# Attention with windowed and global tokens, then expert layers: loads in 64-row halves on ScalarE's queue, gate transposes in the score banks, VectorE copies later

## The chip, the core and the metric

The kernel runs on one core of one Trainium2 chip. The core has five engines with a queue each: TensorE (PE in the profile; PEld is its weight load), VectorE (DVE), ScalarE (ACT), GpSimd (POOL) and SyncE (SP). Each works through its own instructions in order and waits on semaphores of the others. Transfers between HBM and SBUF can be issued by SP, ACT and POOL; the profile shows 16 DMA engines behind them.

The metric is the device time of one execution in microseconds; of several runs the median is taken. Before the change it is 766.53 us, the median of 3 runs (766.46 to 770.74).

## What is computed

Two parts follow one another. The first is an attention over 8 batches of 8 heads: 512 local tokens see the 32 global tokens and a window of 32 tokens to each side, and 32 global tokens see everything. The second sends each of the 4,352 resulting rows to one of 8 experts with a fixed capacity.

```python
s_g = scale * q_g @ concat(k_g, k_l).T             # 32 global queries, all keys
out_g = softmax(s_g) @ concat(v_g, v_l)
s_ll = where(abs(i - j) <= 32, scale * q_l @ k_l.T, -1e9)
s_l = concat(scale * q_l @ k_g.T, s_ll)
out_l = softmax(s_l) @ concat(v_g, v_l)
x = concat(out_g, out_l) as [B*S, H*D]
logits = x @ w_gate                                # greedy assignment, cap = N // E
out[rows of e] = relu(x[rows of e] @ w1[e]) @ w2[e]
```

The diff touches the attention part alone. The expert part starts when all of x and all gate logits are there.

## The kernel before

Inputs are laid out on the host so that a pair of heads is one transfer. The tile `qk` of a pair has 128 partitions, 64 for each head (the head dimension), and holds transposed queries and keys. The tile `vw` has the keys of a window on the 128 partitions, and for each head 16 windows of values with a column of ones. There are 32 pairs, four to a batch. Both tiles have 6 buffers.

The work of a batch is a list of units: two `Local` units for each pair (one for each head) and two `Glob` units (one for four heads). Their order is pair 0, pair 1, Glob 0, pair 2, pair 3, Glob 1, in the last batch pair 0, Glob 0, Glob 1, pairs 1 to 3. There are 80 units. A unit goes through four stages:

- `a`: scores by matmul into PSUM tiles called S (4 buffers). A pair does both of its heads at once with 64 small matmuls (line 160); a Glob does 16 (line 183).
- `e`: on DVE, four passes over the scores that add the mask and find the extreme (line 114), then on ACT four exponentials (line 117). A Glob has two DVE reductions and three exponentials.
- `c`: transposes of the probabilities on PE into PSUM tiles T (2 buffers; line 122, for a Glob line 212), and an evacuation to SBUF by `evac`, which gives three of four to ACT (line 241) and every fourth to DVE (line 243).
- `d`: matmuls with the values into PSUM tiles O (2 buffers; line 131, for a Glob line 222), and on DVE the division by the sum.

The order is written out by hand in one loop (line 327). Iteration i issues, in this order: loads, stores that have come due, `a` of unit i+2 (if it begins a pair or is a Glob), `c` of unit i, `e` of unit i+2, `d` of unit i-1, and then one or more gate steps of an earlier batch. Since every engine keeps program order, what is issued first on an engine runs first there.

Loads before: `load_qk` issues on SP and `load_v` on POOL, whole tiles of 128 partitions. Three qk and two vw tiles are issued ahead of the loop, and the `while` at line 333 then issues as many as the pair index of unit i+2 plus 4 allows, the Globs counting as later pairs. A load whose buffer is still in use waits on its queue, SP or POOL.

The gate: for each finished batch, four steps transpose 128-column blocks of the attention output (`gate_x`, line 249), one multiplies with the gate weights (`gate_m`, line 255) and one transposes back and sums into the logits (`gate_l`, line 264). Before the change the transposes of `gate_x` land in O tiles, except in the last batch, where they land in S tiles.

Of the kernel before, what the change touches and what calls it, by code (L numbers as in the profile page):

```python
# [8 lines left out]
F32 = mybir.dt.float32  # L9
# [9 lines left out]
B, H, SL, SG, D = 8, 8, 512, 32, 64  # L19
S = SL + SG  # L20
# [5 lines left out]
NB = SL // 128  # L26
NW = SL // 32
NP = H // 2
QW = SL + SG
KW = 27 * 32  # L30
# [33 lines left out]
def attention(ctx, tc, A, consts, xd, ident, L, nbatch, rt=None):  # L64
    nc = tc.nc
    ac = ctx.enter_context(tc.tile_pool(name="ac", bufs=1))
    ld = ctx.enter_context(tc.tile_pool(name="ld", bufs=3))
    wk = ctx.enter_context(tc.tile_pool(name="wk", bufs=3))
    ps = ctx.enter_context(tc.tile_pool(name="ps", bufs=2, space=PSUM))

    G = [(b, g) for b in range(nbatch) for g in range(2)]
    qk, vw, xs = {}, {}, {}

    def load_qk(b, p):
        t = ld.tile([128, QW + KW], F32, name="qk", bufs=6)
        nc.sync.dma_start(t, A["qk"][b, p])
        qk[b, p] = t

    def load_v(b, p):
        t = ld.tile([128, 2, NW, D + 1], F32, name="vw", bufs=6)  # L80
        nc.gpsimd.dma_start(t.rearrange("p h w d -> p (h w d)"), A["vw"][b, p])
        vw[b, p] = t

    pg = [ac.tile([128, 6, 128], F32, name=f"pg{i}") for i in range(2)]
    mask = ac.tile([128, NB, 128], F32, name="mask")
# [1 line left out]
    P = [(b, p) for b in range(nbatch) for p in range(NP)]  # L87
# [3 lines left out]
    wt = ps.tile([128, NB, 128], F32, name="T", bufs=2)  # L91
    for _ in range(WARM):
        nc.tensor.matmul(wt[:, 0, :], warm, warm, start=True, stop=True)
    load_qk(0, 0)
    nc.sync.dma_start(mask.rearrange("p a b -> p (a b)"), A["mask"])
    nc.sync.dma_start(ident, A["ident"])
    for i in range(2):
        nc.gpsimd.memset(pg[i], 0.0)
    load_v(0, 0)
    load_qk(0, 1)  # L100
    nc.sync.dma_start(wg.rearrange("p a b -> p (a b)"), A["wg"])
    load_v(0, 1)
    load_qk(0, 2)
    later = []

    class Local:
# [3 lines left out]
        def e(s):  # L110
            s.p = wk.tile([128, NB, 128], F32, name="p", bufs=4)
            nm = wk.tile([128, NB], F32, name="nm", bufs=4)
            for c in range(NB):
                nc.vector.tensor_tensor_reduce(s.p[:, c, :], s.st[:, c, :], mask[:, c, :], -SCALE, BIG,  # L114
                                               ALU.add, ALU.min, nm[:, c:c + 1])
            for c in range(NB):
                nc.scalar.activation(s.p[:, c, :], s.p[:, c, :], AF.Exp, bias=nm[:, c:c + 1], scale=-1.0)  # L117

        def c(s):
            t = ps.tile([128, NB, 128], F32, name="T", bufs=2)  # L120
            for c in range(NB):
                nc.tensor.transpose(t[:, c, :], s.p[:, c, :], ident)  # L122
            s.pt = wk.tile([128, NB, 128], F32, name="pt", bufs=3)
            evac(s.pt, t)

        def d(s):
            b, q, h = s.b, s.q, s.h
            o = ps.tile([128, NB, D + 1], F32, name="O", bufs=2)
            for c in range(NB):
                for r in range(4):  # L130
                    nc.tensor.matmul(o[32 * r:32 * r + 32, c, :], s.pt[:, c, 32 * r:32 * r + 32],  # L131
                                     vw[b, q][:, h, 4 * c + r, :], start=True, stop=True)
            ls = wk.tile([128, NB], F32, name="ls", bufs=4)
            nc.vector.tensor_scalar(ls, o[:, :, D], 1e-9, None, op0=ALU.add)
            nc.vector.reciprocal(ls, ls)
            if q + h == 0:
                xs[b] = wk.tile([128, NB, DM], F32, name="xs", bufs=2)
            hd = D * (2 * q + h)
            nc.vector.tensor_tensor(xs[b][:, :, hd:hd + D], o[:, :, 0:D],
                                    ls[:, :, None].to_broadcast([128, NB, D]), op=ALU.mult)  # L140
            if q == NP - 1 and h == 1:
                later.append(lambda: nc.sync.dma_start(
                    ap_of(xd, (b * S + SG) * DM, [[DM, 128], [128 * DM, NB], [1, DM]]), xs[b]))
# [19 lines left out]
    class Glob:  # L163
# [43 lines left out]
        def c(s):  # L207
            s.pt = wk.tile([128, 6, 128], F32, name="pgt", bufs=2)
            for lo, n in ((0, 4), (4, 2)):
                t = ps.tile([128, NB, 128], F32, name="T", bufs=2)  # L210
                for k in range(n):
                    nc.tensor.transpose(t[:, k, :], s.p[:, lo + k, :], ident)  # L212
                evac(s.pt[:, lo:lo + n], t[:, :n])

        def d(s):
            b, g = s.b, s.g
# [17 lines left out]
            later.append(put)  # L234

    nev = [0]

    def evac(dst, src):
        nev[0] += 1
        if nev[0] % 4 < 3:  # L240
            nc.scalar.activation(dst, src, AF.Copy)
        else:
            nc.vector.tensor_copy(dst, src)

    def gate_x(src, xt, c, spare):
        t = ps.tile([128, NB, 128], F32, name="S" if spare else "O", bufs=4 if spare else 2)
        n = src.shape[1]
        for k in range(n):
            nc.tensor.transpose(t[:, k, :], src[:, k, c * 128:(c + 1) * 128], ident)  # L249
        evac(xt[:, c, :n * 128], t[:, :n].rearrange("p a b -> p (a b)"))  # L250

    def gate_m(xt, n):
        lt = ps.tile([128, 512], F32, name="O", bufs=2)
        for c in range(4):
            nc.tensor.matmul(lt[32 * c:32 * c + 32, :n * 128], wg[:, c, :], xt[:, c, :n * 128],
                             start=True, stop=True)
        ltc = wk.tile([128, 512], F32, name="ltc", bufs=2)
        evac(ltc[:, :n * 128], lt[:, :n * 128])
        return ltc

    def gate_l(ltc, J, n):
        t = ps.tile([128, NB, 4, 32], F32, name="T", bufs=2)
        for k in range(n):
            nc.tensor.transpose(t[:, k].rearrange("p a b -> p (a b)"), ltc[:, k * 128:(k + 1) * 128], ident)
        nc.vector.tensor_reduce(L[:, J:J + n, :], t[:, :n, :, 0:8].rearrange("p k c e -> p k e c"),
                                axis=AX.X, op=ALU.add)

    def gate_units(b, src, J, n):
        xt = []

        def go(c):
            if c == 0:
                xt.append(wk.tile([128, 4, 128 * n], F32, name=f"xt{n}", bufs=2))
            if c < 4:
                gate_x(src(), xt[0], c, b == nbatch - 1)
            elif c == 4:
                xt.append(gate_m(xt[0], n))
            else:
                gate_l(xt[1], J, n)
        return [lambda c=c: go(c) for c in range(6)]  # L280
# [9 lines left out]
    units, heads = [], {}  # L290
# [8 lines left out]
    for b in range(nbatch):  # L299
# [3 lines left out]
        lo = gate_units(b, lambda b=b: xs[b], 4 * b, NB)  # L303
# [5 lines left out]
        else:  # L309
            for k, f in enumerate(lo):  # L310
                extra.setdefault(s0 + (k if b == nbatch - 2 else GS[k]), []).append(f)
            if gl:
                extra.setdefault(s0 + 2, []).append(lambda b=b: load_gx(b // 4))
                for k, f in enumerate(gl):
                    extra.setdefault(s0 + 10 + k, []).append(f)
    nl = [3]

    def pairidx(u):
        if isinstance(u, Local):
            return u.b * NP + u.q  # L320
        return u.b * NP + 2 * u.g + 1

    nu = len(units)
    first = rt.setup(slice(0, 28)) if rt else None
    LA = 2
    due = []
    for i in range(-LA, nu + 3):
        if rt and i == 2:
            rt.load()
        if rt and i == 12:  # L330
            rt.prepare()
        if i + LA < nu:
            while nl[0] < len(P) and nl[0] <= pairidx(units[i + LA]) + 4:
                load_qk(*P[nl[0]])
                load_v(*P[nl[0] - 1])
                nl[0] += 1
                if nl[0] == len(P):
                    load_v(*P[-1])
            while later and due[0] <= i:
                later.pop(0)()  # L340
                due.pop(0)
            if i + LA in heads:
                heads[i + LA].a()
        if 0 <= i < nu:
            units[i].c()
        if i + LA < nu:
            units[i + LA].e()
        if 1 <= i <= nu:
            units[i - 1].d()
        while len(due) < len(later):  # L350
            due.append(i + 2 if i < nu - 10 else i)
        while i >= nu - 10 and later:
            later.pop(0)()
            due.pop(0)
        for f in extra.get(i, []):
            f()
        if rt and i >= nu - 3:
            for _ in range(6):
                next(first, None)
# [45 lines left out]
class Routing:  # L405
# [6 lines left out]
    def load(s):  # L412
        s.cf = s.consts.tile([128, CF], F32, name="cf")
        s.nc.sync.dma_start(s.cf, s.A["cf"])
# [586 lines left out]
```

## Time and profile before

| | |
|---|---|
| median of 3 runs | 766.53 us (766.46 to 770.74) |
| the profiled execution | 772.81 us |
| its span, first to last instruction | 771.0 us |
| PE busy | 680.0 us, 88% |
| DVE busy | 478.1 us, 62% |
| ACT busy | 319.1 us, 41% |
| POOL busy | 130.2 us, 17% |
| moved by DMA | 120.37 MB |

The profiled execution is one run, 6.3 us longer than the median. Times inside it are counted from its first instruction. The profile has these views: busy time of each engine; the span in 40 slices; the DMA queues; the chain of waits that ended last; groups of equal instructions with their mean time; waits by engine and by what ended them; a timeline; and windows, where for any stretch the busy time of each engine, the number of its instructions (x), the granted clock of PE (PEclk, 1.00 is full speed), the busy share of the 16 DMA engines and what they moved stand in one row. "Issue" as the cause of a wait means that the engine waited for nothing that the profile shows.

### The profile page before, as it was taken

How to read it: one execution, taken by the hardware profiler on the slowest of the kernel's cores; microseconds unless marked ns; L12 is line 12 of the kernel's file. 1: busy time of each engine (PE TensorE's matmuls, PEld its weight loads, DVE VectorE, ACT ScalarE, POOL GpSimd, SP SyncE). 2: the span in 40 equal slices, each digit the busy share in tenths (PEclk: the TensorE clock that was granted, in tenths of full speed). 3: DMA queues.
4: the chain of work that ended last, by engine and by line, in shares of the span. 5: the costliest groups of instructions: out<-in, count | busy, mean ns of one | idle time of the engine just before them, and what ended most of it. 6: DMA issues, size and time to landing. Idle time of an engine off the chain costs nothing.

```text
span 771.0 us, 23101 instructions
## 1 busy us (share of the span) xinstructions
PE 680.0 (88%) x9788; PEld 543.9 (71%) x9788; DVE 478.1 (62%) x1742; ACT 319.1 (41%) x823; POOL 130.2 (17%) x150
## 2 busy tenths in 40 slices
PE   6768898888889428999999999999999999989997
PEld 5446665556657217968877977877877886977985
DVE  2566566566657678877777676776776775542410
ACT  3447566565657104434333333342423433442420
POOL 2000010010000013043042033024015014411001
PEclk8889899899999759999999999999999999999999
DMA  9985587776841124062062054045035035513001
GB/s 348 413 336 227 225 318 305 259 288 269 310 169 23 57 103 174 2 249 86 2 260 76 2 186 149 3 130 191 14 111 198 29 111 184 178 45 134 22 14 44
DMA packets 27815, 120.37 MB, mean 156 GB/s; under 512 B 6208, under 2 KB 6464, under 8 KB 19520
## 3 DMA queue, kind: packets, MB, share of 16 engines
q0 software_dynamic: 14848, 85.47, 30.0%
q1 hardware_dynamic: 12864, 33.43, 11.4%
q8 instruction: 77, 1.26, 0.7%
q14 instruction: 26, 0.21, 0.1%
HBM read 101.06 MB, written 17.83 MB: 154 GB/s over the span
## 4 chain that ended last, share of the span: by engine, by line
PE 74%; DVE 15%; issue 7%; ACT 2%; DMA 2%; SPq 0%; POOLq 0%; DVEq 0%; ACTq 0%
PE Y L885 23%; PE H L857 18%; PE S L160 5%; PE T L122 5%; PE O L131 5%; PE R L469 4%; DVE r_G L401 3%; DVE w2l L401 3%; PE S L183 2%; PE H L732 2%; PE O L249 2%; PE O L222 2%; PE Y L875 2%; DVE r_pm L401 2%; PE T L212 1%
## 5 line engine op out<-in xcount | busy, mean ns | idle before, releaser
L857 PE MATMUL H<-xh,w1h 128*128 128x272 f32 x512 | 151.2, 295 | 8.0 <-DVE hl L401 7.8
L857 PE MATMUL H<-xh,w1l 128*128 128x272 f32 x512 | 150.5, 294 | 0.0
L857 PE MATMUL H<-xl,w1h 128*128 128x272 f32 x512 | 150.0, 293 | 0.0
L859 ACT ACTIVATE hh<-H 128x272 fp32r<-128x272 f32 x128 | 50.9, 398 | 136.9 <-PE H L857 120.4
L857 PEld LDWEIGHTS H<-xh,w1h 128*128 128x128 f32 x512 | 96.4, 188 | 12.5 <-DVE hl L401 7.1
L885 PE MATMUL Y<-w2h,hh 128*128 128x512 f32 x256 | 103.8, 405 | 0.0
L885 PE MATMUL Y<-w2h,hl 128*128 128x512 f32 x256 | 102.9, 402 | 0.0
L885 PE MATMUL Y<-w2l,hh 128*128 128x512 f32 x256 | 102.5, 400 | 0.0
L857 PEld LDWEIGHTS H<-xl,w1h 128*128 128x128 f32 x512 | 96.5, 188 | 0.7
L857 PEld LDWEIGHTS H<-xh,w1l 128*128 128x128 f32 x512 | 96.4, 188 | 0.4
L117 ACT ACTIVATE p<-p,nm 128x128 f32<-128x128 f32 x256 | 81.3, 393 | 33.3 <-DVE nm L114 33.3
L114 DVE CUSTOM_DVE_ANT_0 p<-S,mask 128x128 f32<-128x128 f32 x256 | 58.6, 285 | 31.1 <-PE S L160 30.1
L401 DVE SCALAR_TENSOR_TENSOR hl<-H,hh 128x272 fp32r<-128x272 f32 x128 | 54.0, 434 | 22.2 <-ACT h L861 11.4
L401 DVE TENSOR_TENSOR w2l<-w2r,w2h 128x512 fp32r<-128x512 f32 x64 | 42.6, 688 | 38.5 <-ACT w2h L709 38.3
L739 POOL DMA_INDIRECT out_dram<-y,idx x40 | 38.9, 973 | 162.7 <-ACT y L830 105.9
L830 ACT ACTIVATE y<-Y 128x512 f32<-128x512 f32 (+1 forms) x40 | 23.4, 594 | 102.9 <-PE Y L885 71.0
L160 PE MATMUL S<-qk 64*32 64x128 f32 x2048 | 43.3, 293 | 18.8 <-issue 14.0
L885 PEld LDWEIGHTS Y<-w2h,hh 128*128 128x128 f32 x256 | 48.1, 188 | 16.5 <-issue 6.9
L131 PE MATMUL O<-vw,pt 128*32 128x65 f32 x2048 | 47.0, 233 | 12.3 <-issue 9.3
L885 PEld LDWEIGHTS Y<-w2h,hl 128*128 128x128 f32 x256 | 48.1, 188 | 10.5 <-issue 0.6
L885 PEld LDWEIGHTS Y<-w2l,hh 128*128 128x128 f32 x256 | 48.3, 189 | 9.6
L693 POOL DMA_INDIRECT w1r<-in_w_dram,widx x16 | 15.6, 976 | 232.8 <-DVE r_a L401 126.8
(160 smaller groups left out, 1125.4 us busy)
## 6 DMA issues: line engine op xcount, KB each, us to landing
vw<-in_vw_dram POOLq DMA_DIRECT2D x32, 1040.0 KB
qk<-in_qk_dram SPq DMA_DIRECT2D x32, 704.0 KB, 8.5
xd<-xs SPq DMA_DIRECT2D x8, 1024.0 KB, 4.8
xd<-xg SPq DMA_DIRECT2D x64, 8.0 KB, 6.1
xg<-xd,idx POOLq DMA_INDIRECT x40
out_dram<-y,idx POOLq DMA_INDIRECT x40
cf<-in_cf_dram SPq DMA_DIRECT2D x1, 512.0 KB, 27.6
gx<-xd SPq DMA_DIRECT2D x8, 64.0 KB, 4.0
```

The lines of the kernel that those rows point to most:

```text
L114: nc.vector.tensor_tensor_reduce(s.p[:, c, :], s.st[:, c, :], mask[:, c, :], -SCALE, BIG, ALU.add, ALU.min, nm[:, c:c + 1])
L117: nc.scalar.activation(s.p[:, c, :], s.p[:, c, :], AF.Exp, bias=nm[:, c:c + 1], scale=-1.0)
L122: nc.tensor.transpose(t[:, c, :], s.p[:, c, :], ident)
L131: nc.tensor.matmul(o[32 * r:32 * r + 32, c, :], s.pt[:, c, 32 * r:32 * r + 32], vw[b, q][:, h, 4 * c + r, :], start=True, stop=True)
L160: nc.tensor.matmul(u.st[32 * r:32 * r + 32, c, :], t[hp, 32 * j:32 * j + 32], t[hp, k0:k0 + 128], start=True, stop=True)
L401: return op(*args, **kw)
L469: s.nc.tensor.matmul(out, *args, **kw)
L739: nc.gpsimd.indirect_dma_start(out=out, out_offset=bass.IndirectOffsetOnAxis(ap=rt.idx[ph][:n, t:t + 1], axis=0), in_=y[:n], in_offset=None)
L830: nc.scalar.activation(y[:n], p[:n], AF.Copy)
L857: nc.tensor.matmul(p, w[d][:, fs], x[:, d, q], start=(d + k == 0), stop=(d + k == 5))
L859: nc.scalar.activation(hh[:, f, q], p, AF.Relu)
L885: nc.tensor.matmul(p, h[:, f, q], w[f], start=(f + k == 0), stop=(f + k == 9))
```

## The change

Three things are changed, all in the attention.

1. Loads. Whole tiles are still loaded ahead of the loop (three qk, two vw), all of them now issued by SP. In the loop no `while` decides any more: each Local unit of pair p issues, on ACT's queue, one half (64 partitions) of the qk tile of pair p+3, ahead of the `c` of that iteration, and one half of the vw tile of pair p+2, behind the exponentials. The unit of head 0 loads partitions 0 to 63, that of head 1 partitions 64 to 127. Globs issue no loads. POOL loads nothing in the attention any more.
2. `gate_x` uses S tiles in every batch.
3. `evac` can hold a DVE copy back: those of stage `c` are issued behind the `e` of the same iteration instead of ahead of it. Copies on ACT stay where they are.

```diff
+    def load(n, eng, i, half=None):
+        b, p = P[i]
+        if half in (None, 0):
+            if n == "qk":
+                qk[b, p] = ld.tile([128, QW + KW], F32, name="qk", bufs=6)
+            else:
+                vw[b, p] = ld.tile([128, 2, NW, D + 1], F32, name="vw", bufs=6)
+        r = slice(0, 128) if half is None else slice(64 * half, 64 * half + 64)
+        t = qk[b, p] if n == "qk" else vw[b, p].rearrange("p h w d -> p (h w d)")
+        eng.dma_start(t[r], A[n][b, p, r])
...
-    load_qk(0, 0)
+    load("qk", nc.sync, 0)
...
-    load_v(0, 0)
-    load_qk(0, 1)
+    load("qk", nc.sync, 1)
+    load("vw", nc.sync, 0)
...
-    load_v(0, 1)
-    load_qk(0, 2)
+    load("qk", nc.sync, 2)
+    load("vw", nc.sync, 1)
...
-            evac(s.pt, t)
+            evac(s.pt, t, True)
...
+    held = []
+
+    def evac(dst, src, hold=False):
         nev[0] += 1
         if nev[0] % 4 < 3:
             nc.scalar.activation(dst, src, AF.Copy)
+        elif hold:
+            held.append(lambda: nc.vector.tensor_copy(dst, src))
         else:
             nc.vector.tensor_copy(dst, src)
 
-    def gate_x(src, xt, c, spare):
-        t = ps.tile([128, NB, 128], F32, name="S" if spare else "O", bufs=4 if spare else 2)
+    def gate_x(src, xt, c):
+        t = ps.tile([128, NB, 128], F32, name="S", bufs=4)
...
+    def ahead(u, n, k):
+        if isinstance(u, Local) and u.b * NP + u.q + k < len(P):
+            load(n, nc.scalar, u.b * NP + u.q + k, u.h)
+
     for i in range(-LA, nu + 3):
...
         if i + LA < nu:
-            while nl[0] < len(P) and nl[0] <= pairidx(units[i + LA]) + 4:
-                load_qk(*P[nl[0]])
-                load_v(*P[nl[0] - 1])
-                nl[0] += 1
-                if nl[0] == len(P):
-                    load_v(*P[-1])
...
             if i + LA in heads:
                 heads[i + LA].a()
+            ahead(units[i + LA], "qk", 3)
         if 0 <= i < nu:
             units[i].c()
         if i + LA < nu:
             units[i + LA].e()
+            ahead(units[i + LA], "vw", 2)
+        while held:
+            held.pop(0)()
         if 1 <= i <= nu:
             units[i - 1].d()
```

More of the change, by code (lines that the diff above doesn't have):

```diff
@@ L72, in attention @@
     qk, vw, xs = {}, {}, {}
[L74 to L82, printed above, removed]
+    def load(n, eng, i, half=None):
[8 more added lines that the diff above has]
+        eng.dma_start(t[r], A[n][b, p, r])
     pg = [ac.tile([128, 6, 128], F32, name=f"pg{i}") for i in range(2)]
@@ L212, in c @@
                     nc.tensor.transpose(t[:, k, :], s.p[:, lo + k, :], ident)
-                evac(s.pt[:, lo:lo + n], t[:, :n])
+                evac(s.pt[:, lo:lo + n], t[:, :n], True)
         def d(s):
@@ L236, in attention @@
     nev = [0]
-    def evac(dst, src):
+    held = []
+    def evac(dst, src, hold=False):
         nev[0] += 1
@@ L274, in go @@
             if c < 4:
-                gate_x(src(), xt[0], c, b == nbatch - 1)
+                gate_x(src(), xt[0], c)
             elif c == 4:
@@ L315, in attention @@
                     extra.setdefault(s0 + 10 + k, []).append(f)
[L316 to L321, printed above, removed]
     nu = len(units)
```

## The prediction

> **What bounds the kernel now.** I read the page first (span, busy shares, queues), then windows along the span to part attention from experts, then the chain and the waits for PE, and last PE's timeline where a wait had no visible cause. The first rows are the page's: span, PE, the queue named instruction, the two load groups.
>
> ```profile
> span 771.0 us, 23101 instructions
> PE 680.0 (88%) x9788; PEld 543.9 (71%) x9788; DVE 478.1 (62%) x1742; ACT 319.1 (41%) x823; POOL 130.2 (17%) x150
> ...
> q8 instruction: 77, 1.26, 0.7%
> ...
> vw<-in_vw_dram POOLq DMA_DIRECT2D x32, 1040.0 KB
> qk<-in_qk_dram SPq DMA_DIRECT2D x32, 704.0 KB, 8.5
> ```
>
> The windows: the attention (to about 260), the experts, the attention without its first and last part, then a stretch almost free of transfers, a long one full of them, and one with 0.90.
>
> ```profile
> 0.00:260.00 260.00, 211.84 (x5756) 154.03 (x5756) 157.34 (x881) 147.38 (x415) 18.62 (x38) 0.92 0.69 263
> 260.00:771.00 511.00, 468.19 (x4032) 389.90 (x4032) 320.80 (x863) 171.73 (x408) 111.53 (x112) 0.97 0.28 102
> 12.00:250.00 238.00, 199.41 (x5553) 144.55 (x5537) 149.25 (x838) 140.99 (x399) 13.67 (x26) 0.92 0.70 267
> 228.00:246.00 18.00, 17.59 (x543) 13.17 (x543) 11.66 (x69) 13.04 (x35) 0.00 (x0) 1.00 0.20 64
> 18.00:44.00 26.00, 17.75 (x542) 12.93 (x549) 14.77 (x81) 12.42 (x37) 1.06 (x2) 0.86 1.00 409
> 97.00:121.00 24.00, 20.65 (x644) 14.88 (x645) 16.71 (x94) 16.40 (x46) 1.38 (x3) 1.00 0.90 344
> ```
>
> In 260 us of attention PE is busy 211.8; DVE (157) and ACT (147) have room. The experts' 511 us are not touched. PE's pace is what differs: 127 matmuls take 4.21 us in the quiet stretch (18.00 x 127/543), 6.09 in the full one, 4.73 at 0.90, and 5.44 on average over 12 to 250. So the attention is bound by PE, and PE is slowed while transfers run. PE's waits, and those of ACT and DVE that the change aims at:
>
> ```profile
> PE S L160 <- issue: 14.0, 8, 2.8
> PE O L131 <- issue: 9.3, 6, 2.5
> PE O L249 <- issue: 5.0, 2, 2.8
> PE O L222 <- issue: 3.7, 2, 3.3
> ...
> PE S L160 <- DMA qk<-in_qk_dram: 4.5, 1, 4.5
> ...
> PE O L249 <- ACT xt L241: 1.7, 1, 1.7
> ...
> ACT pt L241 <- PE T L122: 49.0, 32, 5.2
> ACT p L117 <- DVE nm L114: 33.3, 21, 5.3
> DVE pt L243 <- PE T L122: 21.7, 16, 5.1
> ```
>
> The four "issue" rows sum to 32.0 us, the largest loss. PE's timeline shows where they fall.
>
> ```profile
> 43.55 1.91 PE L160 MATMUL S<-qk 64*32 64x128 f32 x57 [2.22 <-issue]
> 45.39 1.12 PE L122 MATMUL T<-ident,p 128*128 128x128 f32 x4
> 46.44 1.15 PE L222 MATMUL O<-vw,pgt 128*32 128x65 f32 x48
> 47.52 0.66 PE L122 MATMUL T<-ident,p 128*128 128x128 f32 x4
> 48.11 0.43 PE L131 MATMUL O<-vw,pt 128*32 128x65 f32 x14
> 49.66 0.50 PE L131 MATMUL O<-vw,pt 128*32 128x65 f32 x18 [1.13 <-issue]
> 50.09 0.66 PE L249 MATMUL O<-ident,xs 128*128 128x128 f32 x4
> 50.68 1.12 PE L183 MATMUL S<-qk 64*32 64x512 f32 x16
> 51.73 0.66 PE L122 MATMUL T<-ident,p 128*128 128x128 f32 x4
> 52.32 0.66 PE L131 MATMUL O<-vw,pt 128*32 128x65 f32 x32
> 52.91 1.06 PE L160 MATMUL S<-qk 64*32 64x128 f32 x53
> 56.69 0.44 PE L160 MATMUL S<-qk 64*32 64x128 f32 x11 [2.71 <-issue]
> ```
>
> PE stops in the middle of groups (after 14 of 32, after 53 of 64) whose tiles are there already, and at even distance: 57+4+48+4+14 = 127 matmuls, then 18+4+16+4+32+53 = 127. With their weight loads that is 254 instructions, and the page's 77 packets of the instruction queue for 2 x 9788 PE instructions are 254 each. PE waits for its own next block of instructions, which a transfer brings and which comes late when the DMA engines are full. The rows also show the clock fall with such gaps (0.86 over 18 to 44, 1.00 in the quiet stretch). [...]
>
> **The change part by part.**
>
> *Loads, how many and when.* Before, two pairs come in one burst; after, each Local unit adds a half of qk and a half of vw. Bytes stay: in the loop 29 x 704 + 30 x 1040 KB = 52.9 MB, in 118 transfers, and ahead of it 4.7 MB. If halves move as fast as whole tiles, about 410 GB/s, they need 129 us of 238 and leave gaps in which instruction blocks come in time.
>
> *Loads, how wide.* A half covers 64 partitions. The trace has one kind of load narrower than 128, gx, 32 rows each, issued behind the last stores of xg at 245. Three windows over it, and one over whole tiles:
>
> ```profile
> 245.00:245.60 0.60, 0.60 (x33) 0.43 (x32) 0.60 (x7) 0.27 (x1) 0.00 (x0) 1.00 0.60 154
> 245.60:246.20 0.60, 0.60 (x21) 0.51 (x10) 0.40 (x4) 0.60 (x3) 0.00 (x0) 1.00 0.75 178
> 246.20:246.80 0.60, 0.60 (x9) 0.43 (x8) 0.57 (x3) 0.60 (x4) 0.00 (x0) 1.00 0.52 113
> ...
> 188.00:194.00 6.00, 6.00 (x185) 4.42 (x178) 4.20 (x21) 3.48 (x11) 0.00 (x0) 1.00 1.01 414
> ```
>
> GB/s over DMA share is what fully busy engines would move: 257, 237 and 217 for gx, 410 for whole tiles. Narrow loads keep the same engines busy for nearly twice as long per byte. Rows of gx are short (2 KB), so this is a bound and not a price; from above it is 410. I take 217, the row with the least of the staggered start. Then the loop's loads need 52.9/0.217 = 244 us, more than the stretch of 238 in which they must fit: the transfers become the bound. [...]
>
> The end of attention then follows from the last load. In the last batch Glob 1 comes third and needs the vw of pair 3, which is issued one and two iterations ahead of it; all that follows `d` of that Glob comes after the last landing. Today:
>
> ```profile
> 239.51 0.89 PE L222 MATMUL O<-vw,pgt 128*32 128x65 f32 x48
> ...
> 258.09 0.67 PE T L264 x4
> ```
>
> (the timeline, then the chain): from that Glob to the end 19.3 us, attention ends at 258.8. After: 13 us for the start (4.7 MB at 410 is 11.4, and 1.5 to issue and land), 244, and 19.3: 276. That is **+17 us**. With 237 GB/s it is 255 (-4 us), with 257 it is 238 (-21). If transfers fill the engines throughout and only PE's pace counts, the full stretch gives 5553/127 x (6.09-5.44) = +28.
>
> *Issue on ACT.* 118 issues. ACT shows none before; SP's qk issues are the nearest:
>
> ```profile
> L76 SPq DMA_DIRECT2D qk<-in_qk_dram x32: 328/385/560, 0.8 to 204.0; - x32
> ```
>
> 118 x 0.385 = 45 us of ACT's queue. Behind each stand an evacuation or exponentials, and PE's `c` and `d` wait for these. ACT is busy 147 of 260 and waits 49.0 for T and 33.3 for nm; 147 + 45 = 192 fits. I take 0: the waits cover it. Without that cover it would cost up to 45. No wait is added in practice: the buffers that the halves fill were read three pairs before. SP and POOL lose waits; POOL has nothing else there, and stores on SP go out earlier, from -1 to 0 us.
>
> *Start.* The first six vw loads no longer compete with qk. PE waited 4.5 us for the second qk; ahead of it now stand 704+256+64 KB: some 3 us earlier. As transfers bound the end, I take 0 (from -4.5 to 0).
>
> *DVE copies later.* A copy waiting for T no longer holds up the score passes: up to 21.7 us of DVE's wait. Held copies come four passes later, with `d` an iteration off. DVE is not the bound: 0 (-21.7 to the same again, 16 waits of 1.4).
>
> *Gate transposes in S.* PE's wait of 1.7 for an evacuation in O can go; S keeps four buffers for one more user, and the same wait could arise once in each of 8 batches: 0 (-1.7 to +14).
>
> Sum: +17 us on the profiled 772.8, 789.8. The profiled run is 6.3 above the median of the runs (766.5); against that median **784 us**.
>
> **The rivals.**
>
> *Faster: halves keep the full rate.* One mechanism: short bursts leave gaps, blocks of instructions come in time. For it: 129 us of transfers in 238, quiet pace 4.21, pace 4.73 even at a share of 0.90. Against it: the gx rows. Price: from 5.44 to 4.5 per 127 matmuls, 43.7 x 0.94 = -41, 3 us back for the late vw of the last Glob: -38, 728. It decides from 242 GB/s for halves on: 13 + 219 + 19.3 = 251 is over 1% ahead of today's 258.8.
>
> *Slower by ACT.* Halves are fast, but 45 us of issue land between PE's transposes and the evacuations: for it, PE and ACT hand work to and fro (49.0 and 33.3 of waits); against it, ACT has 113 idle us of 260. If half of the 45 shows, +22, 789. It decides when issue doesn't run beside ACT's own work.
>
> *It does nothing.* Halves move at 237 GB/s, the last landing comes 4 us before today's pace, and gaps gained and lost cancel: 766. For it: the middle gx row.
>
> **How the numbers follow.** My case 48 in 100 (42 slower by over 1%, 6 within), slower by ACT 8, nothing 10, faster 34. One per cent is about what a measurement of this kernel can tell from no change. So faster 0.34, same 0.16, slower 0.50. My case alone has a range of 763 (237 GB/s) to 808: the pace of the full stretch, +28, 14 more if the late S and T waits of the bounds above come on top. The faster case reaches from 755 to 715. With 728 to 808, about 10 in 100 are left out below and 8 above.
>
> **What would show it.** Right: in windows of the attention a DMA share near 1 with 200 to 240 GB/s and not 410; PE waits put down to qk, vw or issue in most units; PEclk below 0.92; the attention ending near 276. Wrong: a share well under 0.8 with gaps in each unit, issue waits under 10 us in all and a pace near 4.5; or halves at over 260 GB/s with the share near 1. For ACT: ACT groups idle little, PE waiting for pt or p. For the copies: ACT's 33.3 us of waiting for nm falls. For the S banks: no PE wait before line 249 but for xs.

## The result and the profile after

The change makes the kernel slower by 10.9%. The changed kernel takes 851.16 us in the median (845.93 to 857.57, 4 runs), the kernel before 766.73 us on the same chip (766.46 to 770.74, 4 runs). The ratio is 1.1092, with a 95% interval from 1.1005 to 1.1178. The profiled execution took 849.57 us. Below, each ratio compares a kernel with runs of the kernel before made together with it, so it can differ a little from the quotient of two medians.

The first rows are those of the page after: span, PE and POOL, two of the DMA queues, the loads (now on ACT's queue, L83) and the stores of xs.

```profile
span 847.8 us, 23122 instructions
...
PE 707.4 (83%) x9788; PEld 558.4 (66%) x9788; DVE 479.7 (57%) x1742; ACT 320.7 (38%) x823; POOL 114.4 (13%) x118
...
q10 hardware_dynamic: 9440, 52.86, 28.0%
...
q8 instruction: 77, 1.26, 0.7%
...
vw<-in_vw_dram ACTq DMA_DIRECT2D x60, 520.0 KB, 7.9
qk<-in_qk_dram ACTq DMA_DIRECT2D x58, 352.0 KB, 7.6
...
xd<-xs SPq DMA_DIRECT2D x8, 1024.0 KB, 9.6
```

The loads of the loop are the 118 transfers and 52.86 MB that were counted beforehand. PE has the same 9,788 matmuls. PE's timeline shows where the attention ends now: at 314.89 the Glob of the last batch goes on (L223, which was L222), having waited for the last vw, and the transposes of the last gate step (L268) end at 336.3.

```profile
314.89 1.02 PE L223 MATMUL O<-vw,pgt 128*32 128x65 f32 x44 [3.09 <-DMA vw<-in_vw_dram]
...
335.67 0.66 PE L268 MATMUL T<-ident,ltc 128*128 128x128 f32 x4 [0.43 <-ACT ltc L243]
```

Before, that end was at 258.8. The attention has grown by 77.5 us, the span by 76.8; the expert part took 512 us before and 511 after. So all of the loss is in the attention. The windows of the changed kernel show its transfers (the last three columns are PEclk, DMA share and GB/s):

```profile
13.00:315.00 302.00, 213.91 (x5217) 148.79 (x5221) 141.85 (x779) 135.16 (x381) 0.00 (x0) 0.83 0.90 209
...
16.00:240.00 224.00, 153.41 (x3808) 107.18 (x3807) 104.18 (x580) 98.44 (x278) 0.00 (x0) 0.82 0.93 214
...
196.00:212.00 16.00, 11.10 (x341) 8.07 (x338) 8.91 (x51) 9.77 (x28) 0.00 (x0) 1.00 1.03 220
```

Before, full DMA engines moved 414 GB/s (188 to 194 in the rows ahead of the prediction). Now they move 220 at a share of 1.03 (a share of 1 or a little more is engines that are all busy). The 224 us from 16 to 240 hold 3,808 matmuls at a granted clock of 0.82; before, 238 us held 5,553 at 0.92.

PE's and ACT's waits in the attention (engine and line, what was waited for, us in all, times, longest):

```profile
PE O L132 <- issue: 30.8, 12, 6.7
...
PE O L223 <- issue: 12.8, 4, 5.6
...
PE S L161 <- issue: 6.3, 7, 1.7
...
PE S L184 <- issue: 3.4, 1, 3.4
...
PE T L213 <- issue: 2.8, 1, 2.8
...
PE O L132 <- ACT pt L243: 16.7, 6, 6.5
...
PE O L223 <- DMA vw<-in_vw_dram: 3.1, 1, 3.1
...
PE S L161 <- DMA qk<-in_qk_dram: 2.9, 2, 2.8
...
ACT pt L243 <- issue: 13.2, 3, 8.2
...
ACT pt L243 <- DMA xd<-xs: 9.1, 1, 9.1
```

PE's issue waits grew from 32.0 us to 56.1. They still fall inside groups of matmuls whose tiles are there. One of them alone lasts 6.68 us; PE ran 127 matmuls between the stop before it, which ends at 104.24, and this one, and 125 to 127 or a multiple of that lie between all 25 stops, the distance of before:

```profile
106.73 0.65 PE L132 MATMUL O<-vw,pt 128*32 128x65 f32 x28
114.06 0.43 PE L132 MATMUL O<-vw,pt 128*32 128x65 f32 x4 [6.68 <-issue]
```

For the loaded tiles themselves PE waits little: the two rows above and two smaller ones sum to 8.6 us. The reader is to see two things that go together: loads that take nearly twice the engine time for each byte (220 GB/s at a share of 1.03 against 414 at 1.01), and PE, whose issue waits at that distance, read in the prediction as waits for its own blocks of instructions, sum to 56.1 us and not 32.0 while the DMA engines are busy 0.93 of the time (0.70 before).

### The profile page after: what moved, and what is told of

The parts are those of the page before. It is cut to its first block, busy times and chain, and to the rows that moved or that the text cites. A ratio compares the mean times of both kernels' runs of the same rounds, so it can differ in the third digit from the quotient of the medians.

```text
span 847.8 us, 23122 instructions
## 1 busy us (share of the span) xinstructions
PE 707.4 (83%) x9788; PEld 558.4 (66%) x9788; DVE 479.7 (57%) x1742; ACT 320.7 (38%) x823; POOL 114.4 (13%) x118
## 3 DMA queue, kind: packets, MB, share of 16 engines
q10 hardware_dynamic: 9440, 52.86, 28.0%
## 4 chain that ended last, share of the span: by engine, by line
PE 42%; DVE 8%; ACT 2%; issue 2%; DMA 1%; POOLq 0%; ACTq 0%; DVEq 0%
PE Y L885 21%; PE H L857 15%; DVE w2l L401 3%; PE R L469 3%; PE H L732 2%; DVE r_G L401 2%; PE Y L875 2%; ACT w2h L709 1%; DVE r_pm L401 1%; DVE hl L401 1%; DMA xg<-xd,idx 0%; PE Y L891 0%; DVE r_ce L401 0%; DMA out_dram<-y,idx 0%; DVE w1l L401 0%
## 5 line engine op out<-in xcount | busy, mean ns | idle before, releaser
L132 PE MATMUL O<-vw,pt 128*32 128x65 f32 x2048 | 53.8, 250 | 49.5 <-issue 30.8
L132 PEld LDWEIGHTS O<-vw,pt 128*32 128x32 f32 x2048 | 39.9, 126 | 60.0 <-issue 36.9
L243 ACT ACTIVATE pt<-T 128x512 f32<-128x512 f32 x47 | 28.0, 595 | 95.7 <-PE T L123 44.7
L161 PE MATMUL S<-qk 64*32 64x128 f32 x2048 | 47.4, 302 | 11.5 <-issue 6.3
```

Source lines behind the costliest of these rows:

```text
L161: nc.tensor.matmul(u.st[32 * r:32 * r + 32, c, :], t[hp, 32 * j:32 * j + 32], t[hp, k0:k0 + 128], start=True, stop=True)
```

## The experiments

Three theories stood against each other at first. The loss comes from the width of the transfers (64 partitions), from their place on ACT, or from the fixed places in the order, which may leave the transfer queues dry. Twelve kernels were run. Line numbers differ by one or two between them, by eight in the one that leaves loads out.

**Halves by columns, on ACT.** The same number of transfers of the same size at the same places, but each covers all 128 partitions and half of the columns.

```diff
-        r = slice(0, 128) if half is None else slice(64 * half, 64 * half + 64)
+        w = t.shape[1] // 2
+        r = slice(0, 2 * w) if half is None else slice(w * half, w * half + w)
-        eng.dma_start(t[r], A[n][b, p, r])
+        eng.dma_start(t[:, r], A[n][b, p, :, r])
```

> The loads of the changed kernel are still halves issued by ACT at the same places and in the same number, but each half is now half the columns of all 128 partitions instead of 64 partitions. Theory W (width): 64-partition transfers move at half rate (the trace after shows 215 to 222 GB/s at a DMA share of 1.02 to 1.03 where whole tiles gave 410), and that rate binds the attention. Then this kernel falls to 735 to 775 us, with over 300 GB/s in the attention. Theory Q (queue): what costs is the place, ACT's queue, where each issue waits for the transfer eight places back and holds exponentials and evacuations behind it. Then it stays above 815 us.

Measured: 786.86 us, ratio 1.0235 [1.0199, 1.0271], between the two ranges and above that of theory W. Most of the loss goes away with the shape of the halves alone; some 2% stays. From 16 to 240 full engines now move 265/0.80 = 331 GB/s, stores included:

```profile
16.00:240.00 224.00, 178.98 (x4877) 126.78 (x4879) 131.52 (x734) 123.80 (x353) 0.00 (x0) 0.92 0.80 265
```

**Halves by rows, on SP and POOL.** The changed kernel with the loads at the same places, but qk issued by SP and vw by POOL.

```diff
-            load(n, nc.scalar, u.b * NP + u.q + k, u.h)
+            load(n, nc.sync if n == "qk" else nc.gpsimd, u.b * NP + u.q + k, u.h)
```

> The changed kernel with its 64-partition halves at the same places, but issued as before the change: qk by SP, vw by POOL. ACT issues no loads. Theory W: the rate of about 217 GB/s stays and the attention with it, the last loads land no sooner than at 255 us, and the time stays between 780 and 850 us. Theory Q: without issues on ACT the time falls to 775 us or less.

Measured: 858.19 us, 1.1191 [1.1150, 1.1232], above the range of 780 to 850. ACT issues no load here, and the loss is all there. So the place on ACT isn't what makes the changed kernel slow.

**Halves by columns, on SP and POOL.** Both edits together.

> Both at once: halves by columns, over all 128 partitions, issued by SP (qk) and POOL (vw) at the places of the change. Theories W and Q both expect it below the kernel before if regular small loads keep PE's instruction blocks in time: 725 to 760 us. If bursts were not what delayed those blocks, it stays within 1% of the kernel before, 759 to 774, with issue waits of PE near the 32 us of before.

Measured: 769.77 us, 1.0028 [0.9997, 1.0058]. With ACT free and a rate near that of whole tiles (from 20 to 60 full engines move 346/0.91 = 380 GB/s, in the kernel before 362/0.91 = 398), small regular loads are as good as the bursts of before, and not better. The gain that was hoped for, blocks of instructions that come in time between short bursts, didn't come. PE's waits in this kernel sum to 33.2 us of issue, as before:

```profile
PE S L162 <- issue: 16.3, 9, 3.3
...
PE O L133 <- issue: 9.6, 9, 2.7
...
PE S L254 <- issue: 5.3, 2, 3.4
...
PE O L224 <- issue: 2.0, 2, 1.2
```

**The kernel before, with the gate in S and the held copies alone.** The loads stay as they were; the edits of `gate_x`, `evac` and `held` are those of the change.

> The kernel before with the other two parts of the change alone: gate transposes in S tiles, DVE copies held behind the score passes; loads as before. Theories W and Q: within 1% of before, 759 to 774 us. Theory S (a score bank or a late copy holds PE): above 785 us, with PE waits on S tiles or on DVE copies of over 15 us.

Measured: 763.40 us, 0.9928 [0.9894, 0.9962], the fastest of the kernels that load everything. Two of its wait rows answer to rows of before: ACT's wait for nm fell from 33.3 us to 20.5, and the gate's transposes wait for no evacuation, but for xs (and 1.0 us of issue).

```profile
ACT p L117 <- DVE nm L114: 20.5, 12, 5.1
...
PE S L253 <- DVE xs L139: 2.4, 1, 2.4
```

**The kernel before, with each load in two halves by rows.** Engines, places and order of the loads stay as before.

```diff
-        nc.sync.dma_start(t, A["qk"][b, p])
+        for r in (slice(0, 64), slice(64, 128)):
+            nc.sync.dma_start(t[r], A["qk"][b, p, r])
...
-        nc.gpsimd.dma_start(t.rearrange("p h w d -> p (h w d)"), A["vw"][b, p])
+        for r in (slice(0, 64), slice(64, 128)):
+            nc.gpsimd.dma_start(t.rearrange("p h w d -> p (h w d)")[r], A["vw"][b, p, r])
```

> The kernel before in everything but one thing: each whole load is issued as two loads of 64 partitions, one behind the other, by the same engines at the same places. Theory W alone (all of the loss is the width): the time is that of the changed kernel, 835 to 865 us. Theory P (the rate of 217 GB/s costs some 40 us, and the rest comes because loads at fixed places, a few ahead, leave the transfers without work at times): 800 to 825 us, with a DMA share near 1 until the last load.

Measured: 868.88 us, 1.1256 [1.1180, 1.1332], a little above the range. Loads in halves by rows make the kernel before as slow as the changed one, or slower, with none of the fixed places. This window of it shows about the rate of the changed kernel (208/0.89 = 234 GB/s for full engines, 230 there) and the same small breaks (a share of 0.89), though all loads are queued as early as their buffers allow:

```profile
16.00:300.00 284.00, 192.32 (x4561) 137.00 (x4562) 124.15 (x697) 117.97 (x330) 25.36 (x50) 0.79 0.89 208
```

**Whole tiles at the fixed places, on ACT and on SP and POOL.** Head 0 loads the whole qk tile, head 1 the whole vw tile.

```diff
-        if isinstance(u, Local) and u.b * NP + u.q + k < len(P):
-            load(n, nc.scalar, u.b * NP + u.q + k, u.h)
+        if isinstance(u, Local) and u.b * NP + u.q + k < len(P) and u.h == (n == "vw"):
+            load(n, nc.scalar, u.b * NP + u.q + k)
```

> The changed kernel with whole tiles on ACT: qk of pair p+3 at the place of head 0, vw of pair p+2 at that of head 1, so 59 issues in place of 118. The halves by columns on ACT gave 786.9, the same on SP and POOL 769.8. Theory N (number: each issue takes 0.47 us of ACT, and each of the eight completion semaphores comes round the sooner the more transfers there are): 766 to 778 us. Theory C (the place on ACT costs whatever the number): 782 to 792 us.

> As the kernel with whole tiles at fixed places, but issued by SP (qk) and POOL (vw). Theories W, P, N: no half-width transfers and no issue on ACT, so 757 to 770 us, near the kernel before with the other two parts alone (763.4). Only if fixed places cost time by themselves, over 775.

Measured: on ACT 785.93 us, 1.0123 [1.0031, 1.0215]; on SP and POOL 771.24 us, 0.9971 [0.9935, 1.0008], 1 us above the range (the kernel before took 771.39 beside them). With whole tiles the fixed places cost nothing. Half as many issues on ACT give the same median as the 118 of the halves by columns; the ratios are 1.0123 and 1.0235, but their intervals overlap, so the number of issues doesn't stand out as the cause.

**The kernel before without most of its loads.** Pairs from 6 on compute with the tiles of the first six: 26 of the 32 loads of qk and of vw are left out (`load_v` has the same edit as `load_qk`), and what those pairs compute is not the reference's. It bounds what all loads cost in the kernel before.

```diff
     def load_qk(b, p):
+        i = P.index((b, p))
+        if i >= 6:
+            qk[b, p] = qk[P[i % 6]]
+            return
```

> The kernel before without the loads of the pairs from the seventh on: they compute with the tiles of the first six, which leaves out 26 of 32 loads each of qk and vw. It measures what any arrangement of the loads could gain. If transfers delay PE's instruction blocks and with them its clock (the reading of the profile before): the pace of the quiet stretch, 4.2 us for 127 matmuls, from about 40 us on, so 715 to 735 us, and under 10 us of issue waits of PE behind 40 us. If the gaps have another cause: above 750.

Measured: 741.83 us, 0.9595 [0.9500, 0.9689], 29.6 us less than before; a larger gain was expected. In a long stretch PE has the full clock at a DMA share of 0.15 (columns as above), and the issue waits of its attention rows are 9.7 us:

```profile
40.00:220.00 180.00, 166.34 (x5055) 121.86 (x5057) 138.07 (x774) 128.02 (x363) 0.00 (x0) 1.00 0.15 51
```

```profile
PE O L230 <- issue: 3.6, 2, 3.3
PE O L139 <- issue: 3.3, 1, 3.3
PE S L168 <- issue: 2.5, 2, 1.5
...
PE T L272 <- issue: 0.3, 1, 0.3
```

So about 30 us (24 to 39 by the interval, from two runs) is all that any better way of loading could win here.

**Halves by alternate rows, on ACT.** Why are 64 rows slow: because they are few, or because they lie on one side? The changed kernel with every second partition in a half, even ones for head 0 and odd ones for head 1.

```diff
-        r = slice(0, 128) if half is None else slice(64 * half, 64 * half + 64)
+        r = slice(0, 128) if half is None else slice(half, 128, 2)
```

> The changed kernel with one edit: a half is every second partition (even ones for head 0, odd ones for head 1) instead of the lower or the upper 64. Count, size and places of all transfers stay: 64 rows of 5,632 or 8,320 bytes each, on ACT. Theory R (64 rows are too few for the engines, whichever they are): rows keep taking twice as long, loads at 215 to 225 GB/s when the engines are full, 840 to 860 us. Theory L (the loss comes from all rows of a half lying on one side of the 128 partitions): full rate of over 400 GB/s in full stretches, and the time of halves by columns on ACT, 780 to 792 us.

Measured: 791.02 us, 1.0226 [1.0150, 1.0302], the time of the halves by columns. Rows of the same number and length now move at the rate of whole tiles (414 GB/s at a share of 1.01). From 20 to 24 such loads take 98.3% of the engines' time, and full engines move 412 GB/s; the second row is a long stretch:

```profile
20.00:24.00 4.00, 2.64 (x102) 1.91 (x101) 2.70 (x17) 2.07 (x7) 0.00 (x0) 1.00 1.01 412
```

```profile
16.00:240.00 224.00, 179.05 (x4944) 126.19 (x4944) 134.47 (x744) 125.13 (x356) 0.00 (x0) 0.93 0.80 268
```

From 16 to 240 the engines are busy 0.80 of the time and move 268 GB/s, 335 for full engines; the changed kernel has 0.93 and 214, which is 230. Which 64 rows a transfer covers is what counts, and not that they are 64.

**Stores on POOL.** What are the 2% on ACT? The instruction list of the changed kernel names a reason. From the ninth on, every transfer on SP and ACT waits for one of eight completion semaphores that both queues take in turn, that is, for an earlier transfer to have landed. Four rows of ACT's order and one of SP's, by their number in the queue (equal neighbours count as one):

```
ACT 11 L83 DMA vw<-in_vw_dram 64x2080 [waits DMAHW6_49]
ACT 12 L83 DMA qk<-in_qk_dram 64x1408 [waits DMAHW7_49]
ACT 13 L243 ACTIVATE pt<-T 128x512 [waits PE_49]
ACT 15 L83 DMA vw<-in_vw_dram 64x2080 [waits DMAHW0_49]
SP  14 L143 DMA xd<-xs 128x4x512 [waits DMAHW7_49,DVE_49]
```

A store of SP waits for DVE as well, and a load of ACT whose turn comes behind it holds the evacuation that follows on ACT. In the kernel with halves by columns on ACT the waits show it:

```profile
ACT pt L244 <- DMA xd<-xs: 31.9, 4, 9.4
...
PE O L133 <- ACT pt L244: 15.2, 7, 3.6
...
ACT p L119 <- DMA xd<-xs: 8.2, 1, 8.2
...
ACT pt L244 <- DMA xd<-xg: 7.5, 1, 7.5
```

The edit issues the stores of xs and xg on POOL, first with the halves by columns.

```diff
-                later.append(lambda: nc.sync.dma_start(
+                later.append(lambda: nc.gpsimd.dma_start(
...
-                    nc.sync.dma_start(ap_of(xd, b * S * DM + (4 * g + r) * D, [[DM, SG], [1, D]]),
+                    nc.gpsimd.dma_start(ap_of(xd, b * S * DM + (4 * g + r) * D, [[DM, SG], [1, D]]),
```

> Halves by columns on ACT (786.9 us) with one edit: the stores of xs and xg are issued by POOL instead of SP, so they no longer take a turn among the completion semaphores that SP's and ACT's transfers share. Theory V (ACT is held because a load waits for its turn behind a store of SP, which itself waits for DVE): ACT's waits put down to xs and xg (47.6 us in all) go, and the time falls to 766 to 776 us. Theory I (the issues themselves take ACT's time): the waits move elsewhere and the time stays at 782 to 790 us.

Measured: 770.55 us, 0.9955 [0.9910, 1.0000]. The three rows with xd are gone and the fourth is down to 1.6 us; the stores wait where they hold nobody, on POOL, and ACT's largest wait is again for PE:

```profile
POOL xd L144 <- DVE xs L141: 52.9, 6, 10.0
ACT pt L244 <- PE T L124: 49.4, 37, 5.2
```

So the 118 issues themselves cost nothing that can be measured. Their turn behind the stores costs some 16 us by the medians; by the ratios, 1.0235 and 0.9955, it is 2.8% or 21 us, since the kernel before took 773.76 beside these runs and 766.65 beside the others. The same edit was then made in the changed kernel and in the one with whole tiles on ACT.

> The changed kernel as it is (851.2 us), with the stores of xs and xg issued by POOL instead of SP. If the turns that its loads take behind the stores cost time of their own beside the half rate of the loads: 825 to 840 us. If the half rate alone sets the end, so that a held ACT only waits where it would have waited for the transfers: 845 to 862 us, as with the loads on SP and POOL (858.2).

> Whole tiles on ACT, 59 issues in place of 118 (785.9 us), with the stores of xs and xg issued by POOL instead of SP. If the shared turns are what a load on ACT costs, also with half as many of them: 766 to 776 us, as with halves by columns (786.9 to 770.6). If something else does it for whole tiles, since ACT's waits put down to xs and xg were only 6.5 us there: 780 to 790 us.

Measured: in the changed kernel 845.76 us, 1.0941 [1.0892, 1.0989], at the edge of the second case. Against 1.1092, from another set of runs, that is 1.5 of 10.9%; the rest of the loss stays. With whole tiles on ACT 782.37 us, 1.0150 [1.0097, 1.0202], no gain: what whole tiles cost on ACT is not the turns behind stores, and stays open.

## Why the prediction was wrong

The direction was right: slower, by the half rate of loads of 64 adjoining partitions (222 GB/s, as worked out below), which keep the transfer engines busy for 0.90 of the attention. The time was not: +17 us forecast on the profiled execution, +77 measured, and 851 lies far above the range's end of 808.

**What held.** The rate did. From 16 to 300 of the changed kernel, the DMA queues show (packets, MB, share of 16 engines):

```profile
q10 hardware_dynamic: 9074, 50.61, 80.4%
...
q1 hardware_dynamic: 6125, 8.40, 10.0%
...
q8 instruction: 38, 0.62, 1.1%
```

The loads moved 50.61 MB in 0.804 x 284 = 228 us of the engines' time, 222 GB/s where 217 was taken. With that rate the 52.86 MB need 238 us; 244 was forecast. The gx rows were the right row for the price, though gx is 32 rows and short, so that the agreement to 2% is partly luck. The rate goes with which 64 partitions a half covers (412 GB/s at a share of 1.01 for every second one, against 220 at 1.03 for adjoining ones); why it does, no run shows.

**The step that failed: the sum "13 + 244 + 19.3 = 276".** Start and tail were nearly right: the last vw is there at 314.9 and the tail took 21.4 us. The middle had 244 us and took 302 (13 to 315). It counted the loads alone, as if nothing else moved and the engines never stopped. The rows give both missing terms. Other queues took 10.0% and 1.1% of the time, some 34 us in 302: stores, gx, the expert part's first table, instructions. And the share of 0.90 in the window from 13 to 315 leaves 30 us in which engines stood still. So 238 + 34 + 30 = 302. The second term could have been had from the trace of before, where stores and instruction blocks take the same engines (from 0 to 220 the queue named instruction has 38 packets and 1.1% of their time); the third was put at zero without a reason, because a bound was taken to be busy all the time.

The trace shows when the breaks come. From 16 to 300, the issues and landings of ACT's loads put at most two of them under way for 80 us, and 25 of the 29.5 us that idle engines come to lie there; with three or more under way the share is 0.98 and above. So the engines stand still mostly because the next loads are not issued yet. One such place, in ACT's order and in a window near its end:

```profile
56.63 0.47 ACTq L83 DMA_DIRECT2D qk<-in_qk_dram  x1
...
63.56 0.47 ACTq L83 DMA_DIRECT2D vw<-in_vw_dram  x1
64.08 0.61 ACTq L83 DMA_DIRECT2D qk<-in_qk_dram  x1
```

```profile
60.00:64.00 4.00, 3.22 (x33) 1.73 (x36) 2.03 (x6) 0.00 (x0) 0.00 (x0) 0.50 0.53 189
```

For 7 us ACT issued no load: the next one had its turn behind a store of xs, which landed at 63.54 by the trace's record of that semaphore. (ACT's wait of 9.1 us for xd in the rows of the profile after is another such place.) These turns are not the only reason: with the stores on POOL the share from 16 to 300 is 0.92, as in the changed kernel. In the kernel before with halves by rows (0.89) it is POOL's loads that wait, for Globs to be done with the buffers:

```profile
POOL vw L83 <- PE O L224: 240.5, 12, 32.4
```

The loads thus follow the work of PE, directly or by way of a store, and PE's issue waits, read as waits for instruction blocks that pass the same engines (1.1% and 1.0% of their time), are 56.1 us in the changed kernel and 84.4 in this one. That each holds up the other fits the rows; no run separates the two.

**The ends of the range.** The upper end, +28 and 14 more, came from "only PE's pace counts" in full stretches. PE lost more than that pace. The stretch that gave it was 26 us long, and the share over the attention of before was 0.70; here the share is 0.93 on average over 224 us, the clock is 0.82, and the issue waits of the whole attention are 56.1 us. At the other end, 237 GB/s gives 255.5 by the same sum, so -3.3 us and not -4; nothing hangs on that.

**"No wait is added in practice".** Wrong as a statement: each load on ACT waits for its turn among eight semaphores, beside the wait for its buffer that was looked at. With full-rate halves this costs 16 to 21 us (786.86 to 770.55 with the stores moved); in the changed kernel the ratio fell from 1.1092 to 1.0941. The price of the issues, 0 between 0 and 45, was right, though each took 0.47 us on ACT and not 0.385: 770.55 (0.9955) with 118 issues on ACT, 769.77 (1.0028) without any.

**"Stores on SP go out earlier, from -1 to 0".** This looked at when they go out and not at when they land: from issue to landing a store of xs took 4.8 us before and 9.6 after, and a load on ACT whose turn comes behind it waits for the landing. The row of before, from its first 220 us:

```profile
xd<-xs SPq DMA_DIRECT2D x6, 1024.0 KB, 4.8
```

**Copies and gate banks at 0.** Right to within 1%: together they bring 0.7% (763.40), at the places that were named, ACT's wait for nm and the gate's wait for an evacuation.

**The rivals.** "Faster" had 34 in 100 and was overrated by its price. Its own condition, halves at 242 GB/s or more, was made true by columns (380 on SP and POOL), and the time was 769.77 and not 728: issue waits stayed at 33.2 us. Even where they fell, to 19.7 us with the columns on ACT and to 26.1 with the stores moved as well, the time was no better than before (786.86 and 770.55). Leaving out most loads takes 29.6 us off. So -38 by a better pattern of loading was more than there was to win, or nearly all of it. "Slower by ACT" at 789 is what the columns on ACT show (786.86), but through the turns behind the stores and not through the issues. In the changed kernel the half rate (222 GB/s) outweighs both.

## What to carry to other kernels

A split into the lower and the upper 64 partitions alone cost 12.6% here, in a kernel that was not bound by transfers before (a DMA share of 0.70); a split by columns cost 0.3% on SP and POOL, and on ACT columns cost 2.4% and alternate rows 2.3%. So split a load by columns or by alternate rows. When transfers become the bound, sum everything that uses their engines (stores, instruction blocks: 11% of their time here) and allow for breaks (10% here), which came mostly where the next load was issued late (25 of 29.5 us); loads alone gave 276 where 336 was measured. Before loads are put on a compute engine's queue, list which semaphores they wait for and who else takes turns there, and try the stores that wait for late results on another queue: with halves by columns that took 786.86 us to 770.55, with whole tiles it gained nothing (1.0150).

## What was not expected of the hardware

- Halves of 64 adjoining partitions moved at 220 GB/s with full engines, halves of 64 alternate ones at 412, with equal rows. Two queues of adjoining halves at once (SP and POOL) gained nothing: 858.19 and 868.88 us, against 851.16 with ACT's alone.
- PE's stops, some 127 matmuls apart, lasted up to 6.68 us each (the DMA share from 107 to 114, in that stop, is 1.03), 3.3 in the rows of before. In the four kernels with adjoining halves PE's issue waits were 56 to 84 us, and those for qk and vw 9 to 24.
- Whole tiles on ACT cost 1.5% even when they no longer share turns with stores, while halves by columns there cost nothing (0.9955). No run explains it.
